# A retention block with a feed-forward block behind it: chunk 0's q loaded first, chunk 1 turned around chunk 0's products, chunk 8 turned by VectorE

## The chip, the cores and the metric

The kernel runs on one core of a Trainium2 chip. The metric is the device time of one execution in microseconds (us), lower is better, as the median of several runs. The core has five engines that run side by side, each with its own queue of instructions: TensorE (PE in the profile, with its weight loads as PEld), VectorE (DVE), ScalarE (ACT), GpSimd (POOL) and SyncE (SP), which here only issues transfers. Transfers (DMA) are also issued by ScalarE and GpSimd.

## What is computed

The inputs are q, k and v of 8 batches, 8 heads, 576 positions and 64 values each, a weight w_in of 512 x 2048 and a weight w_out of 2048 x 512, the weights in float64.

```python
scores = scale * np.matmul(q, k.transpose(0, 1, 3, 2))
gamma = 1.0 - 2.0 ** (-5.0 - np.arange(H))
Dmat = np.where(rel >= 0, gamma[:, None, None] ** rel[None, :, :], 0.0)   # rel = query position - key position
attn = np.matmul(scores * Dmat[None], v)             # (8, 8, 576, 64)
x = attn.transpose(0, 2, 1, 3).reshape(4608, 512)    # a row for each token
h = np.maximum(x @ w_in, 0.0)
out = h * h @ w_out                                  # (4608, 512)
```

## The kernel before

**Chunks.** The 4608 tokens are 36 chunks of 128, each of two halves of 64; nine halves make a sequence. A chunk's attention is: load q, k and v; scale q and v by powers of gamma (`scale_q`, `scale_v`); turn q and k, so that the head's 64 values lie along the partitions; multiply them to scores; mask the scores; multiply with v; add what a running state (k times v, summed over what came before) gives; and add this chunk to the state. The state is summed in a PSUM tile `u_ps`, and ScalarE copies it to `u_sb` after each half (`grown`, line 501) before the next half is added to the same tile (lines 538 and 568). The result of a chunk is copied to `room` as columns of x (line 550).

**Two ways of turning.** A chunk below `N_TURN` is turned by TensorE (`turn`: sixteen transposes, line 445, into two PSUM tiles, and two copies out, line 454, by ScalarE and VectorE or by ScalarE alone). A chunk from `N_TURN` on is turned by VectorE (`flip`): one transpose of k and one of q (line 416), each of which turns blocks of 32 x 32, and then sixteen copies of 32 x 256 on ScalarE (line 431), which put the blocks where they belong. The copies wait in a list, `moves`, and `move(count)` takes up to so many from it before each step.

**Order of the work.** Nothing is reordered: each engine runs what the program wrote for it in the order written. The first four chunks and parts of the next are written out by hand. They use `scores_full`, `carry_full` and `retain_full` on whole chunks. In between stands `convert`, which takes single operations of the weights' conversion from 64 bits to float32. A piece of w_in is 128 columns of it: `fetch_raw` issues its load of 512 KB, and six operations convert it: lines 227, 231, 238, 241 and 244 on VectorE, and line 235 on ScalarE, whose result line 241 needs. `first_in` (line 677) multiplies a converted piece with the first 512 tokens; there are sixteen of these, and ScalarE takes each result out of PSUM (line 683) and squares it (line 685). `warm` (line 845) is matmuls without a use.

**The chunk loop.** For each later chunk i, the loop first puts out what is left in `moves` for chunk i, then finishes the attention of chunk i - 1 (`whole`, lines 568, 574, 609, with the scores of the next chunk, line 480), turns chunk i + 1 if it is below `N_TURN`, scales its v on GpSimd, issues loads (`loads`), starts `flip` of chunk i + 2 if that is for VectorE, and then runs some feed-forward steps (`ffn`). Such a pass for i is called round i here. In rounds 5 to 8 the steps are three of `first_in`; before each, ScalarE gets `move`, then a piece is converted, and one of the pending transposes is put on VectorE. In `whole`, ScalarE copies the first half's state (line 501), and TensorE's next line 568 adds the following half to the same PSUM tile.

**Buffers.** q has three, k five and v four (`ld3`, `ld5`, `ld4`). A load waits for the last reader of the buffer that it takes. SP issues all loads in order, apart from chunk 0's k and v, which ScalarE issues.

**The rest.** From 95 us on TensorE works on the feed-forward blocks of 512 tokens with Strassen products (line 717), among the chunks, and from about 485 us on the second layer (line 1063). The change does not touch these.

Of the kernel before, what the change touches and what calls it, by code (L numbers as in the profile page):

```python
# [41 lines left out]
def kernel(  # L42
# [33 lines left out]
    nc = tc.nc  # L76
# [3 lines left out]
    HP = H // 2  # L80
# [10 lines left out]
    N_CH = n_tok // C  # L91
# [48 lines left out]
    def load(i, names="qkv"):  # L140
        if i == 0:
            nc.sync.dma_start(dv, decays)
        got = loaded.setdefault(i, [None] * 3)
        for name, pool, src in (("q", ld3, q), ("k", ld5, k), ("v", ld4, v)):
            if name not in names:
                continue
            t = got["qkv".index(name)] = pool.tile([128, H, D], F32, tag=name, name=f"{name}_ld")

            issue = nc.scalar if i == 0 and name != "q" else nc.sync
            b, c0 = divmod(i * C, S)  # L150
            runs = [(b, c0, slice(0, C))] if c0 + C <= S else [(b, c0, slice(0, CH)), (b + 1, 0, slice(CH, C))]
            for e in range(1 if name == "v" else 2):
                for b, c0, to in runs:
                    at = src[b, :, c0:c0 + to.stop - to.start, :].rearrange("h s d -> s h d")
                    if name == "v":
                        issue.dma_start(t[to], at)
                    else:
                        issue.dma_start(t[to, e * HP:(e + 1) * HP, :], at[:, e::2, :])
# [23 lines left out]
    def rows(half, n=64):  # L182
        return slice(64 * half, 64 * half + n)
# [21 lines left out]
    def fetch_w(j):  # L205
        if j < len(pieces) and wide:
            to = raw_of(j).bitcast(I64)
            if pieces[j][0] == 0:
                nc.sync.dma_start(to.rearrange("p (c f) -> p c f", c=N_DM), piece_src(j))
                return  # L210
            to = to.rearrange("p (o s b c) -> o s p b c", o=2, s=2, b=4)
            for o in range(2):
                for s in range(2):
                    nc.sync.dma_start(to[o, s], piece_src(j)[o, s])
# [94 lines left out]
    def fetch_raw(count):  # L309

        for _ in range(count):
            if n_raw[0] < min(N_W1, n_made[0] + N_RAW):
                fetch_w(n_raw[0])
                n_raw[0] += 1
# [18 lines left out]
    def convert(count):  # L333
        for _ in range(count):
            f = next(w_in_steps, None)
            f and f()
# [41 lines left out]
    def head(hp, e):  # L378
        return 4 * (hp % 2) + 2 * e + hp // 2

    HEADS = [(hp, e, hp // (HP // 2)) for hp in range(HP) for e in range(2)]
# [4 lines left out]
    def clears(half, bank):  # L386

        new = (half, bank) not in clean
        clean.add((half, bank))
        return new  # L390

    def scale_q(i, engine, parts=(slice(0, H),)):
        at = N_PAT + i % N_PAT
        for heads in parts:
            t = loaded[i][0][:, heads, :]
            engine.tensor_tensor(t, t, dv[:, heads, at:at + 1].to_broadcast(list(t.shape)), op=ALU.mult)  # L396
# [1 line left out]

    N_TURN = 9
    ps_t = [None]
    moves = []

    def new_qk(i):
        t = work3.tile([128, 2, HP, C], F32, tag="qk", name="qk")
        st[i]["qT"], st[i]["kT"] = t[:, 0, :, :], t[:, 1, :, :]
        return t
# [19 lines left out]
    def move(count, i=N_CH):  # L428

        while moves and count and moves[0][0] <= i and (moves[0][1] <= done[0] or count == C):  # L430
            nc.scalar.copy(*moves.pop(0)[2:])  # L431
            count -= 1

    def turn_in(i, js=(1, 0)):

        if "p" not in st[i]:
            if i < N_EARLY:
                p = [ps_e.tile([128, 512], F32, tag=f"e{h}", name="t_ps") for h in range(2)]
            else:
                p = [ps_f.tile([128, 512], F32, tag="f", name="t_ps") for h in range(2)]  # L440
            st[i]["p"] = [x.rearrange("p (j d t) -> p j d t", j=2, d=HP) for x in p]
        for j in js:
            for hp in range(HP):
                for h in range(2):
                    nc.tensor.transpose(st[i]["p"][h][:, j, hp, :], loaded[i][j][rows(h), 2 * hp:2 * hp + 2, :],  # L445
                                        ident[rows(h), rows(h)])

    def turn_out(i, engines=(0, 1)):

        p = st[i].pop("p")  # L450
        to = new_qk(i)
        copies = (nc.scalar.copy, nc.vector.tensor_copy)
        for h in range(2):
            copies[engines[h]](to[:, :, :, CH * h:CH * h + CH], p[h])

    def turn(i, engines=(0, 1)):
        turn_in(i)
        turn_out(i, engines)
# [41 lines left out]
    def grown(i, h):  # L500
        nc.scalar.copy(u_sb[(2 * i + h + 1) % 3], u_ps[0])
# [15 lines left out]
    def x_full(hp, e, b):  # L517
        return xp[0][rows(b), e, 0:256].rearrange("p (g t) -> p g t", g=2)[:, hp % 2, :]

    def carry_full(i):  # L520

        xp[0] = ps_x.tile([128, 2, 256], F32, tag="x", name="x_ps", padded_shape=[128, 2, 512])
        clean.clear()
        if i == 0:
            u_ps[0] = ps_u.tile([128, HP, D], F32, tag="u", name="u_ps")
            return
        u = u_sb[2 * i % 3]
        for hp, e, b in HEADS[0:2] + HEADS[4:6] + HEADS[2:4] + HEADS[6:8]:
            nc.tensor.matmul(x_full(hp, e, b), lhsT=u[rows(e), hp, :], rhs=st[i]["qT"][rows(e), hp, :],
                             start=clears(b, e), stop=False, skip_group_check=True)  # L530

    def retain_full(i):

        for hp, e, b in (HEADS[j] for j in (0, 4, 2, 6, 1, 5, 3, 7)):
            nc.tensor.matmul(x_full(hp, e, b), lhsT=st[i]["vs"][:, head(hp, e), :], rhs=st[i]["ret"][:, e, hp, :],  # L535
                             start=clears(b, e), stop=False, skip_group_check=True)
        for hp, e, b in HEADS:
            nc.tensor.matmul(u_ps[0][rows(e), hp, :], lhsT=loaded[i][1][:, 2 * hp + e, :], rhs=st[i]["vs"][:, head(hp, e), :],
                             start=(i == 0 and hp == 0), stop=(hp == HP - 1), skip_group_check=True)
        x_out(i, lambda: grown(i, 1))  # L540
# [256 lines left out]
    def step():  # L797
        n, f, *args = steps.pop(0)
        done[0] += 1
        f(*args)  # L800
        for _ in range(2 if len(transfers) > 2 else 1):
            if transfers and ahead[0] > QUIET:
                transfers.pop(0)[1]()
# [9 lines left out]
    def ffn(i):  # L813

        if steps and steps[0][0] == 0:

            for _ in range((N_W1 - N_EARLY) * C // TOK):
                move(4)
                convert(6)
                for f in flips[:1]:  # L820
                    f()
                del flips[:1]
                step()
            return
        count = N_MP * NP * C // TOK
        while steps and count:
            held[0] = count <= 1

            due = sum(m[0] <= i + 2 for m in moves)
            move(max(2, min(4, -(-due // (count - 1)))) if count > 1 else 0)  # L830
            ahead[0] = count
            busy[0] = len(flips) > 0
            for f in flips[:1]:
                f()
            del flips[:1]
            step()
            count -= 1
        held[0] = busy[0] = False
        ahead[0] = N_DF
# [6 lines left out]

    def loads(i):
        if i + 3 < N_CH:
            load(i + 3, "qk")
        if i + 2 < N_CH:  # L850
            load(i + 2, "v")

    halves = (slice(0, HP), slice(HP, H))
    warm(5)
    scale_q(0, nc.vector, halves)
    turn_in(0, (1,))
    scale_v(0)
    turn_in(0, (0,))
    turn_out(0)
    scale_q(1, nc.vector, halves)  # L860
    load(3)
    fetch_raw(3)
    warm(1)
    scores_full(0)
    turn(1, (0, 0))
    carry_full(0)
    retain_full(0)
    convert(3)
    scores_full(1)
    scale_q(2, nc.gpsimd)  # L870
    carry_full(1)
    retain_full(1)
    convert(3)
    turn(2, (0, 0))
    load(4)
    load(5, "qk")
    fetch_raw(1)
    load(5, "v")
    fetch_raw(1)
    first_in(0, (0,), (0, C))  # L880
# [26 lines left out]
    convert(3)  # L907
    scores(4)
    turn(5, (0, 0))
    load(7, "qk")  # L910
    scale_q(6, nc.gpsimd)
    convert(3)
    step()
# [1 line left out]
    for i in range(N_EARLY + 1, N_CH + 1):  # L915
        move(C, i)
        whole(i - 1)
        if i == N_EARLY + 1:
            convert(4)
        if i + 1 < N_TURN:  # L920
            turn(i + 1, (0, 0))
        if i + 1 < N_CH:
            scale_v(i + 1)
        loads(i)
        if N_TURN <= i + 2 < N_CH:
            flip(i + 2)
        ffn(i - 1)
        for j in range(n_scaled[0], min(i + (4 if i > N_TURN - 4 else 3), N_CH)):
            n_scaled[0] += 1
# [214 lines left out]
    for k in range(N_K + 1):  # L1144
        j = k % NP
# [81 lines left out]
```

## Time and profile before

| | |
|---|---|
| time, median of 3 runs | 931.64 us (931.31 to 931.79) |
| profiled execution | 931.4 us, of which the span of the profile is 929.7 |
| granted TensorE clock | 0.999 |
| PE busy | 922.7 us, 99% of the span |
| DVE, ACT, POOL busy | 756.2, 346.4, 84.3 us |
| ACT copies out of `flip` (line 431) | 432, 173.8 us, 402 ns each |
| DMA moved | 181.29 MB, 195 GB/s over the span |

Times in the views are microseconds from the start of the span. In a row of the timeline the start comes first, then the busy time, the engine, the line of the kernel, the operation, what it writes and reads, and how many instructions the row merges. In square brackets stands how long the engine was idle before it and what released it. TensorE's busy time is modelled at its end, since matmuls overlap, so that intervals between starts say more. Each float32 matmul is recorded twice. The DMA view gives, for the transfers issued in a stretch of time, the time from issue to landing.

### The profile page before, as it was taken

To read this page: it belongs to the slowest core of one execution; us is meant where nothing else is said; L and a number is where in the kernel's file an instruction comes from. 1 tells how busy PE (TensorE), PEld (TensorE's weight loads), DVE (VectorE), ACT (ScalarE), POOL (GpSimd) and SP (SyncE) were. 2 spreads that over 40 slices of the span, in tenths; PEclk is the share of its full clock that TensorE was granted. 3 is DMA by queue.
4 is the path that set the end of the run, shared out by engine and by line. 5 is a ranking of instruction groups with operands and counts; after the bars stand their busy time and mean duration, and the time that the engine had idled before them with its cause. 6 is when DMAs were issued, how large, how long until landed. Compare 5 with 4: busy or idle time off the path is not lost.

```text
span 929.7 us, 21073 instructions
## 1 busy us (share of the span) xinstructions
PE 922.7 (99%) x8548; PEld 830.3 (89%) x8548; DVE 756.2 (81%) x1215; ACT 346.4 (37%) x788; POOL 84.3 (9%) x84
## 2 busy tenths in 40 slices
PE   8999999999999999999999999999999999999998
PEld 7654888888888888888888899999999999999997
DVE  5888798888898888979876587878888888877887
ACT  3457767667676676676711110000000000000000
POOL 3322111121111111211000000000000000000000
PEclk9999999999999999999999999999999999999999
DMA  9998657678666785784379996566666575465523
GB/s 223 223 258 231 169 150 200 165 212 267 166 182 182 261 216 146 224 267 140 115 255 345 381 334 194 145 165 197 175 165 195 151 209 156 116 177 138 151 85 68
DMA packets 297152, 181.29 MB, mean 195 GB/s; under 512 B 194112, under 2 KB 270016, under 8 KB 296160
## 3 DMA queue, kind: packets, MB, share of 16 engines
q1 hardware_dynamic: 292064, 178.81, 66.4%
q10 hardware_dynamic: 4928, 1.08, 0.6%
q8 instruction: 67, 1.10, 0.5%
q14 instruction: 29, 0.24, 0.1%
q0 software_dynamic: 64, 0.07, 0.0%
HBM read 109.39 MB, written 70.52 MB: 194 GB/s over the span
## 4 chain that ended last, share of the span: by engine, by line
PE 98%; DVE 1%; issue 0%; POOL 0%; ACT 0%; POOLq 0%; DVEq 0%
PE h_b L717 18%; PE o_b L1063 17%; PE h_a L717 12%; PE h_c L717 12%; PE o_c L1063 12%; PE o_a L1063 12%; PE h_ps L677 6%; PE x_ps L574 3%; PE sc_ps L480 2%; PE x_ps L609 1%; PE u_ps L568 1%; PE idle_ps L845 0%; PE t_ps L445 0%; PE sc_ps L509 0%; PE x_ps L535 0%; DVE room L513 0%
## 5 line engine op out<-in xcount | busy, mean ns | idle before, releaser
L717 PE MATMUL h_b<-room,w 128*128 128x256 f32 x768 | 181.5, 379 | 0.0
L431 ACT COPY qk<-flip 32x256 f32<-32x256 f32 x432 | 173.8, 402 | 6.7
L717 PEld LDWEIGHTS h_b<-room,w 128*128 128x128 f32 x768 | 145.8, 190 | 20.0 <-DVE room L736 0.2
L717 PE MATMUL h_a<-room,w 128*128 128x256 f32 x512 | 123.9, 385 | 0.0
L717 PE MATMUL h_c<-room,w 128*128 128x256 f32 x512 | 121.0, 379 | 0.0
L717 PEld LDWEIGHTS h_c<-room,w 128*128 128x128 f32 x512 | 97.3, 190 | 13.2
L717 PEld LDWEIGHTS h_a<-room,w 128*128 128x128 f32 x512 | 95.0, 190 | 13.7
L1063 PE MATMUL o_b<-room,w 128*128 128x192 f32 x496 | 90.7, 326 | 0.0
L1076 ACT COPY r<-o_a 128x192 f32<-128x192 f32 x28 | 8.9, 319 | 209.4 <-PE o_a L1063 209.4
L1063 PEld LDWEIGHTS o_b<-room,w 128*128 128x128 f32 x496 | 82.3, 190 | 0.0
L724 DVE SCALAR_TENSOR_TENSOR room<-room 128x512 f32<-128x512 f32 x96 | 67.2, 700 | 3.3
L396 POOL TENSOR_TENSOR q_ld<-q_ld,dv 128x512 f32<-128x512 f32 x34 | 37.8, 1113 | 286.2 <-DMA q_ld<-in_q_dram 240.7
L1063 PE MATMUL o_a<-a,w 128*128 128x192 f32 x352 | 62.6, 326 | 0.0
L1063 PE MATMUL o_b<-s,w 128*128 128x192 f32 x336 | 61.5, 326 | 0.0
L1063 PE MATMUL o_c<-s,w 128*128 128x192 f32 x336 | 61.5, 326 | 0.0
L1063 PE MATMUL o_c<-room,w 128*128 128x192 f32 x336 | 61.5, 326 | 0.0
L677 PE MATMUL h_ps<-room,w 128*128 128x512 f32 (+1 forms) x152 | 57.7, 532 | 0.6 <-DVE w L244 0.5
L1063 PEld LDWEIGHTS o_a<-a,w 128*128 128x128 f32 x352 | 58.1, 190 | 0.1
L1063 PE MATMUL o_a<-room,w 128*128 128x192 f32 x320 | 56.9, 326 | 0.0
L1063 PEld LDWEIGHTS o_b<-s,w 128*128 128x128 f32 x336 | 55.8, 190 | 0.0
L1063 PEld LDWEIGHTS o_c<-s,w 128*128 128x128 f32 x336 | 55.8, 190 | 0.0
L1063 PEld LDWEIGHTS o_c<-room,w 128*128 128x128 f32 x336 | 55.8, 190 | 0.0
(117 smaller groups left out, 1412.6 us busy)
## 6 DMA issues: line engine op xcount, KB each, us to landing
g_dram<-room SPq DMA_DIRECT2D x164, 256.0 KB, 3.8
a<-g_dram SPq DMA_DIRECT2D x30, 512.0 KB, 5.8
room<-g_dram SPq DMA_DIRECT2D x28, 512.0 KB, 5.1
w_dram<-w SPq DMA_DIRECT2D x28, 448.0 KB, 4.4
w<-w_dram SPq DMA_DIRECT2D x7, 1792.0 KB, 9.6
q_ld<-in_q_dram SPq DMA_DIRECT2D x64, 128.0 KB, 4.1
w<-in_moe_w_in_dram SPq DMA_DIRECT2D x16, 512.0 KB, 6.0
w<-in_moe_w_out_dram SPq DMA_DIRECT2D x64, 128.0 KB, 3.4
```

The lines of the kernel that those rows point to most:

```text
L396: engine.tensor_tensor(t, t, dv[:, heads, at:at + 1].to_broadcast(list(t.shape)), op=ALU.mult)
L431: nc.scalar.copy(*moves.pop(0)[2:])
L480: nc.tensor.matmul(st[i]["sc"][e][rows(h), hp, :], lhsT=st[i]["kT"][rows(e), hp, t], rhs=st[i]["qT"][rows(e), hp, t], start=True, stop=Tru ...
L568: return [lambda hp=hp, e=e, b=b: nc.tensor.matmul(u[rows(e), hp, :], lhsT=loaded[i][1][rows(h), 2 * hp + e, :], rhs=st[i]["vs"][rows(h), ...
L574: return [lambda hp=hp, e=e, b=b: nc.tensor.matmul(x_at(hp, e, b, h), lhsT=s["vs"][rows(h), head(hp, e), :], rhs=s["ret"][rows(h), e, hp, ...
L609: m = nc.tensor.matmul(x_at(hp, e, b, h), lhsT=u[rows(e), hp, :], rhs=s["qT"][rows(e), hp, CH * h:CH * h + CH], start=clears(b, e), stop=F ...
L677: nc.tensor.matmul(p, lhsT=w[:, c, :], rhs=xT[0][:, c, :].rearrange("p (h t) -> p h t", h=2)[:, lo:hi, at[0]:at[1]], start=(c == 0), stop= ...
L717: nc.tensor.matmul(p[:, mm, :], lhsT=w[:, c, :], rhs=xs[n][right][:, c, :], start=(j in OPENS and mm == 0 and c == 0), stop=(j in CLOSES a ...
L724: nc.vector.scalar_tensor_tensor(t, t, 0.0, t, op0=ALU.max, op1=ALU.mult)
L1063: nc.tensor.matmul(p, lhsT=w_out[j][:, m, WO_SLOT[right], :], rhs=s["lefts"][left][:, m, :], start=(i in OPENS and m == 0), stop=(i in CLO ...
L1076: nc.scalar.copy(r[:, 0, LEFT], p)
```

## The change

Line numbers in this text are those of the kernel before; behind line 532 the changed kernel's are three higher, from the function `loads` on they differ a little more.

- Chunk 0: ScalarE issues q's two loads instead of k's two and v's one; SP issues k and v behind the decays.
- Chunk 1: VectorE scales half of q, GpSimd the other half. The sixteen transposes are split into two groups of eight: one directly behind chunk 0's scores, one between the fourth and the fifth of the eight products of chunk 0's scores with v. The two copies out go to ScalarE and VectorE instead of ScalarE alone. The first weight piece's six operations are placed two, two and two instead of three and three.
- The load of the fifth weight piece (piece 4) is issued before q, k and v of chunk 5 instead of behind its q and k.
- `loads` issues v with q and k of the same chunk, three chunks ahead; before, v came two chunks ahead. Chunk 7's v likewise.
- `N_TURN` is 8 instead of 9: chunk 8 is turned by VectorE. In rounds 5 to 8 up to five of the waiting copies precede each step instead of four.

```diff
-            issue = nc.scalar if i == 0 and name != "q" else nc.sync
+            issue = nc.scalar if i == 0 and name == "q" else nc.sync
...
-    N_TURN = 9
+    N_TURN = 8
...
-    def turn_in(i, js=(1, 0)):
+    def turn_in(i, js=(1, 0), hps=range(HP)):
...
-            for hp in range(HP):
+            for hp in hps:
...
-    def retain_full(i):
-
-        for hp, e, b in (HEADS[j] for j in (0, 4, 2, 6, 1, 5, 3, 7)):
+    def retain_full(i, inside=lambda: None):
+
+        for j in (0, 4, 2, 6, 1, 5, 3, 7):
+            hp, e, b = HEADS[j]
+            if j == 1:
+                inside()
...
-                move(4)
+                move(5)
...
         if i + 3 < N_CH:
-            load(i + 3, "qk")
-        if i + 2 < N_CH:
-            load(i + 2, "v")
+            load(i + 3)
...
-    scale_q(1, nc.vector, halves)
+    scale_q(1, nc.vector, halves[:1])
+    scale_q(1, nc.gpsimd, halves[1:])
     load(3)
     fetch_raw(3)
     warm(1)
     scores_full(0)
-    turn(1, (0, 0))
+    turn_in(1, (1, 0), (0, 1))
     carry_full(0)
-    retain_full(0)
-    convert(3)
+    retain_full(0, lambda: [turn_in(1, (1, 0), (2, 3)), turn_out(1), convert(2)])
+    convert(2)
     scores_full(1)
     scale_q(2, nc.gpsimd)
+    convert(2)
     carry_full(1)
     retain_full(1)
-    convert(3)
     turn(2, (0, 0))
     load(4)
+    fetch_raw(1)
     load(5, "qk")
-    fetch_raw(1)
     load(5, "v")
     fetch_raw(1)
...
-    load(7, "qk")
+    load(7)
```

## The prediction

> **What bounds the kernel now.** I read the page first: shares of busy time, then the chain that ended last.
>
> ```profile
> PE 922.7 (99%) x8548; PEld 830.3 (89%) x8548; DVE 756.2 (81%) x1215; ACT 346.4 (37%) x788; POOL 84.3 (9%) x84
> PE 98%; DVE 1%; issue 0%; POOL 0%; ACT 0%; POOLq 0%; DVEq 0%
> ```
>
> TensorE is the bound: a change can pay only where TensorE stands or does work it could leave out, and can hurt only where it makes TensorE wait. So I went through TensorE's rows in order of time.
>
> ```profile
> 6.17 0.89 PE L445 MATMUL t_ps<-w,q_ld 64*128 64x64 f32 x8
> 6.99 0.75 PE L845 MATMUL idle_ps<-w 128*128 128x256 f32 x2
> 7.97 1.16 PE L509 MATMUL sc_ps<-qk 64*128 64x128 f32 x16 [0.23 <-DVE qk L454]
> 10.10 1.16 PE L535 MATMUL x_ps<-room,v_ld 128*64 128x128 f32 x16 [0.21 <-DVE room L513]
> 13.69 1.16 PE L535 MATMUL x_ps<-room,v_ld 128*64 128x128 f32 x16 [0.27 <-DVE room L513]
> 16.55 1.16 PE L677 MATMUL h_ps<-room,w 128*128 128x128 f32 x8 [0.51 <-DVE w L244]
> ```
>
> All real waits lie before 17 us and are half a microsecond or less each. After that the timeline is dense, but one edge in it is tight: ScalarE's copy of the state (L501) and the next product into the same PSUM tile (L568), which must not start before the copy has read it.
>
> ```profile
> 41.38 0.37 ACT L501 COPY u_sb<-u_ps 128x256 f32<-128x256 f32 x1
> 41.61 0.28 PE L574 MATMUL x_ps<-qk,v_ld 64*64 64x64 f32 x4
> 41.90 0.27 PE L568 MATMUL u_ps<-v_ld,k_ld 64*64 64x64 f32 x2
> ```
>
> The copy ends at 41.75 and L568 starts at 41.90; later the pairs are 68.28 and 68.42, 81.54 and 81.69. It is always 0.14 to 0.15 us after the copy: if ScalarE is late there, TensorE is late by as much. This is ScalarE ahead of the third pair, in the round that the change touches:
>
> ```profile
> 77.08 0.60 ACT L683 ACTIVATE room<-h_ps 128x512 f32<-128x512 f32 x1 [1.65 <-PE h_ps L677]
> 77.58 1.63 ACT L431 COPY qk<-flip 32x256 f32<-32x256 f32 x4
> 79.23 0.72 ACT L235 ACTIVATE w<-w,exp_bias 128x512 uint32<-128x512 uint32 x1
> 79.86 0.61 ACT L685 ACTIVATE room<-room 128x512 f32<-128x512 f32 x1
> 80.51 0.60 ACT L683 ACTIVATE room<-h_ps 128x512 f32<-128x512 f32 x1
> 81.17 0.37 ACT L501 COPY u_sb<-u_ps 128x256 f32<-128x256 f32 x1
> ```
>
> A block-0 step takes TensorE 3.43 us (L683 starts at 73.65, 77.08, 80.51). ScalarE with four L431 copies, L235, L685 and L683 fills just that: no idle between 77.08 and 81.17. It has nothing left for a fifth copy.
>
> **What the Trainium skill says.** "PSUM — Partial Sum Buffer", section Engine vs sequencer instructions: ScalarE's and VectorE's queues are strict FIFO and matmuls start in program order. The rows above agree: L501 runs only after L683. So a moved copy delays all behind it. "VectorE: DVE Perf Modes", section The three transpose paths: VectorE transposes 32x32 blocks only. The trace agrees: each chunk turned so costs two transposes of 0.70 us and sixteen block copies (L431). "DMA: Bandwidth & Descriptors", section Issuing engines are not separate DMA queues: queues of SP and ScalarE share the same engines. The page's first slices show them 90% busy or more. "SBUF — State Buffer", section SBUF: two separate sides: VectorE and GpSimd exclude each other on a shared port. The trace fits: L231 takes 1.28 us instead of 0.42 at 57.04, beside GpSimd's row at 56.80.
>
> **The change, part by part.**
>
> *Chunk 0's q first.* Now q's second half lands at 6.08 (the DMA view: issued 1.74, 4.3 later), its scaling starts at 6.11, and TensorE's second half of q's transposes at 6.59. k sent by ScalarE at 0.80 and 1.30 landed at 3.49 and 4.77; q will land there. k on SP takes q's old place, behind the decays, but no v runs beside it: I estimate 5.2 (decays, q and k are 584 KB, 2.6 us at the first slice's 223 GB/s, from about 2.0, and half a microsecond of tail), at worst the old 6.08. TensorE can't begin before 5.69, where the warm-up matmuls end. So the 0.28 stall at 6.59 and some 0.13 of restart go: scores(0) moves from 7.97 to about 7.56. With k at 6.08 it gains 0.15.
>
> *Chunk 1 turned around chunk 0's products.* The bytes up to k1 are the same, so k1 still lands at 8.73 and 9.26. Half of q1's scaling leaves VectorE (0.4 us before the masks) for GpSimd. First masks at about 8.7 instead of 9.28, first products at 9.4, second half of the turn, second products, state: 0.5 + 0.4 + 0.5 + 0.6 gives scores(1) at 11.4 instead of 11.66. But step three of the weight piece (L238, 0.7 to 0.9) now stands before chunk 1's masks: 227 and 231 from 11.14, 238 until 12.8, masks at 12.8, where they started before (12.85). In return the piece is ready at 15.5 instead of 16.49. Chunk 2's k lands at 15.41 (issued 10.66, 4.75 later), and the turn of chunk 2 (15.25 now) can't pass it. It ends at 16.05 as before, first_in follows at 16.1 instead of 16.55, and scores(2) waits for ScalarE's two copies until 17.3 instead of 17.64. **Early gain: 0.34.** Bounds: 0 if k0 or q1 comes late, 0.65 if k2 lands without its tail.
>
> *Fifth weight piece ahead of chunk 5.* w4 landed at 35.92 and VectorE waited 0.51 for it, TensorE did not: its product starts at 43.4, and L244 of that piece ends at 40.1. With w4 ahead (2.3 us from 33.59 to 35.92), q5 lands at about 34.8 instead of 32.47 and k5 at 35.9; GpSimd scales q5 until 35.9, and the turn of chunk 5 wants k5 and q5 at 36.0 to 36.3. Nothing, with at most 0.5 of loss. Cover: four h_ps matmuls before it.
>
> *v with q and k.* v comes one chunk earlier; 256 KB, some 1.2 us, stand before the weights from w8 on. The tightest is piece 11: landed 61.94, used by L227 at 63.41; it becomes 63.1 against about 63.6. On SP, v now waits for the products of the chunk whose buffer it takes, just finished on TensorE; behind it stand stores of g, with buffers for two groups. Nothing; bound 0 to 0.5.
>
> *Chunk 8 turned by VectorE.* The chain shows what leaves TensorE:
>
> ```profile
> 69.34 0.64 PE t_ps L445 x16
> 69.98 10.50 PE h_ps L677 x24
> ```
>
> **Gain 0.64.** ScalarE loses two copies (1.09 at 70.06) and gets sixteen of 0.41 a chunk earlier, five a step instead of four. In order: chunk 8's are due 5 in the last step of round 6, then 5, 5 and 1 in round 7, where chunk 9's first 4 follow (now: 0, 0, 4).
>
> Round 6: L683 starts at 63.82 in the trace; + 0.50 + 5 x 0.41 + 0.63 + 0.52 to 0.65 gives the next at 67.5 to 67.7 against 67.25. L501 and so L568 slip by 0.2 to 0.4: **loss 0.3**.
>
> Round 7, from the start S of its first step: round 8 now shows first copies of L431 at S + 0.92 (83.45 against 82.53). Five copies until 2.98, L235 to 3.61, L685 to 4.13, L683 to 4.73, five copies to 6.79, L235 and L685 to 7.94, L683 to 8.54, one copy to 8.95. Chunk 9's copies wait for VectorE's transpose of q: its 241 waits for L235 (7.54), 244 follows at 8.27, the transpose at 8.88 to 9.58. Four copies until 11.3, L235 and L685 to 12.45, L683 to 13.0, then L501. Its present place is S + 10.5 + 0.76 = 11.26. **Loss 1.74**, 1.4 to 2.1 with the longer durations. There is no cover: L568 follows the copy directly. What is late next: nothing; TensorE's pause lets ScalarE catch up. In round 8 ScalarE ends its third step at about 10.8 against 10.4, and chunk 8's second half ends a sequence, so that no L501 comes before its products. VectorE's 1.4 us of new transposes in round 6 lie in its 1.94 idle at 67.2. Piece 12 is ready at S + 5.1 and wanted at 6.86.
>
> **Sum.** -0.34 - 0.64 + 0.3 + 1.74 = +1.06. The profiled execution took 931.4 (span 929.7), so 932.5; the median of the runs shown is 0.24 above it: **932.7**. Whatever moves before 95 us carries through: TensorE is dense to the end.
>
> **Rivals.** *ScalarE's copies stay hidden.* Then only gains are left: -0.98, 930.7. For it: ScalarE is 37% busy in all, and idles 1.36 and 1.65 in round 7. Against it: those 3.0 us, less 0.64 of shorter round, have to hold 15 copies in place of 4 and two wide ones, +3.4. *The start gains far more:* if chunk 2's data come before 14.8 and the copies stay hidden, -0.65 - 0.64 and some further tenths: 930.0, at best 929.5; only there is it faster. *The start gives nothing and the copies cost their upper bound:* 0.4 + 2.1 - 0.64 and 0.3 of waiting for q5 or k0 gives +2.2, 933.8, slower. It decides at L501 more than 2.5 us behind its present place.
>
> **How the numbers follow.** A measurement tells 0.2% (1.86 us) from no change. Likeliest case 62%, hidden copies 16%, large early gain 5%, upper bound with a lost start 17%. Slower by over 0.2% (above 933.5): the last and 8 of the first, 25%. Faster (below 929.8): 5%. Within: 70%. The range takes in the hidden copies and the upper bound: 930.6 to 934.2.
>
> **What would show it.** After: scores(0) near 7.6; the products of chunk 2's first_in near 16.1; no t_ps rows before the third round of h_ps; L501 of round 7 about 2.5 us after the h_ps matmuls of its block end instead of 0.76, with L568 0.15 behind its end; five L431 copies of 0.41 each. I am wrong if L501 keeps its place, if chunk 2's k lands much before 15.4, or if TensorE waits on q5, k5 or a weight piece in the stretch from 35 to 95 us.

## The result, and the profile after

The changed kernel takes 933.5 us (median of 14 runs, 932.51 to 936.25), the kernel before 931.33 us in the same comparison (931.07 to 932.03): a ratio of 1.0023, 95% interval 1.0016 to 1.0031. It is slower by 2.2 us. The interval, 1.5 to 2.9 us, leaves out no change at all, but it takes in the 1.86 us at which the prediction drew its line. The prediction was 932.7 (930.6 to 934.2). Of the single terms some are right and others wrong, as the traces show. The profiled execution of the changed kernel took 933.73, its span is 932.0 (before: 931.4 and 929.7).

First the page of the changed kernel, busy time and the chain that ended last:

```profile
PE 922.5 (99%) x8532; PEld 829.6 (89%) x8532; DVE 762.9 (82%) x1217; ACT 350.8 (38%) x801; POOL 86.4 (9%) x85
PE 94%; DVE 3%; DMA 1%; ACT 1%; issue 1%; POOL 0%; SPq 0%; POOLq 0%; DVEq 0%
```

TensorE's busy time is hardly less (the transposes that it lost are small). Of the chain 4% has gone from TensorE to others. That would be 37 us, and TensorE has lost 2.3: the chain says which way the last releases lead back, not how long TensorE stood. To see where it stood, TensorE's starts of the same matmul are laid side by side in both traces. A positive number means that the changed kernel is later there. The last column is the last matmul.

| matmul of the kernel before at (us) | 16.6 | 40 | 56.7 | 69.9 | 82.5 | 95.0 | 439 | end |
|---|---|---|---|---|---|---|---|---|
| changed kernel | +0.22 | +0.49 | +0.49 | -0.05 | +1.63 | +1.63 | +2.34 | +2.34 |

So four steps: +0.49 at the start, -0.54 in round 6 (0.64 of transposes saved, 0.10 lost), +1.68 at the end of round 7, and +0.71 in the Strassen part after 270 us. The start, in TensorE's, VectorE's and GpSimd's timeline of the changed kernel:

```profile
12.30 1.52 DVE L238 SCALAR_TENSOR_TENSOR w<-w,w 128x512 f32<-128x512 uint32 x1
13.74 1.27 DVE L513 TENSOR_TENSOR room<-sc_ps,room 128x512 f32<-128x512 f32 x2
12.21 1.06 POOL L495 TENSOR_TENSOR v_ld<-v_ld,dv 128x512 f32<-128x512 f32 x1 [3.56 <-DMA v_ld<-in_v_dram]
14.57 1.16 PE L538 MATMUL x_ps<-room,v_ld 128*64 128x128 f32 x16 [0.99 <-DVE room L513]
16.77 1.16 PE L680 MATMUL h_ps<-room,w 128*128 128x128 f32 x8
18.13 1.05 PE L509 MATMUL sc_ps<-qk 64*128 64x128 f32 x14 [0.21 <-ACT qk L454]
```

Scores of chunk 0 begin 0.26 earlier (7.71 for 7.97). But L238 takes 1.52 us, and not the 0.69 that it takes undisturbed, since GpSimd's scaling of v1 began just before it. The masks L513 wait behind it until 13.74 (before: 12.85), and chunk 1's products come at 14.57 instead of 13.69. The weight piece itself is then ready in good time: nothing waits at 16.77. Scores(2) at 18.13 wait for ScalarE's copies of chunk 2's turn, which the late products have delayed (before: 17.64).

Round 7 on ScalarE, and TensorE's next product:

```profile
79.56 1.65 ACT L431 COPY qk<-flip 32x256 f32<-32x256 f32 x4 [0.67 <-DVE flip L416]
81.23 0.72 ACT L235 ACTIVATE w<-w,exp_bias 128x512 uint32<-128x512 uint32 x1
81.86 0.61 ACT L688 ACTIVATE room<-room 128x512 f32<-128x512 f32 x1
82.38 0.58 ACT L686 ACTIVATE room<-h_ps 128x512 f32<-128x512 f32 x1
82.86 0.36 ACT L501 COPY u_sb<-u_ps 128x256 f32<-128x256 f32 x1
83.32 0.27 PE L571 MATMUL u_ps<-v_ld,k_ld 64*64 64x64 f32 x2 [1.46 <-issue]
```

The chain is as predicted: chunk 9's four copies wait for VectorE's transpose, all else queues behind them, L501 starts at 82.86, and TensorE follows 0.10 us after its end.

The last step, +0.71 after 270 us, starts at 261 us, with the scalings of v. First the kernel before, then the changed one:

```profile
261.36 1.06 POOL L495 TENSOR_TENSOR v_ld<-v_ld,dv 128x512 f32<-128x512 f32 x1 [1.66 <-DMA v_ld<-in_v_dram]
261.85 0.69 DVE L736 TENSOR_TENSOR room<-h_b,room 128x512 f32<-128x512 f32 x1 [0.59 <-PE h_b L717]
```

```profile
260.96 1.61 POOL L396 TENSOR_TENSOR q_ld<-q_ld,dv 128x512 f32<-128x512 f32 x1 [11.88 <-DMA q_ld<-in_q_dram]
261.57 1.28 DVE L227 TENSOR_SCALAR w<-w 128x512 uint32<-128x512 uint32 x1
262.53 1.23 POOL L495 TENSOR_TENSOR v_ld<-v_ld,dv 128x512 f32<-128x512 f32 x1
262.77 1.28 DVE L231 TENSOR_SCALAR w<-w 128x512 uint32<-128x512 uint32 x1
263.97 0.68 DVE L739 TENSOR_TENSOR room<-h_b,room 128x512 f32<-128x512 f32 x1
279.77 1.56 PE L720 MATMUL h_b<-room,w 128*128 128x256 f32 x6 [0.24 <-DVE room L739]
```

In the kernel before, the scaling of v waited 1.66 us for its data, and VectorE was through with L227 and L231 (0.41 and 0.42 us) before it; it even stood idle for 0.59. In the changed kernel v is there already, GpSimd scales q and v back to back, and L227 and L231 take 1.28 us each. L739 is then 2.12 later than L736 was in the kernel before, while TensorE is only 1.63 later. VectorE has no idle time in which to make this up, and at 279.77 TensorE waits for it. Between 275 and 279 us L238, L241 and L244 take 3.3 us together in both traces, so that nothing more is lost there. What is left of the 0.71 is lost at matmuls of h_b at 378 and 393 us, 0.2 and 0.1.

### The profile page after: what moved, and what is told of

Read it like the earlier page. It is cut to its first block, busy times and chain, and to the rows that moved or that the text cites. A ratio compares the mean times of both kernels' runs of the same rounds, so it can differ in the third digit from the quotient of the medians.

```text
span 932.0 us, 21034 instructions
## 1 busy us (share of the span) xinstructions
PE 922.5 (99%) x8532; PEld 829.6 (89%) x8532; DVE 762.9 (82%) x1217; ACT 350.8 (38%) x801; POOL 86.4 (9%) x85
## 4 chain that ended last, share of the span: by engine, by line
PE 94%; DVE 3%; DMA 1%; ACT 1%; issue 1%; POOL 0%; SPq 0%; POOLq 0%; DVEq 0%
PE o_b L1065 17%; PE h_b L720 17%; PE h_a L720 12%; PE o_c L1065 12%; PE o_a L1065 12%; PE h_c L720 11%; PE h_ps L680 5%; PE x_ps L577 3%; PE sc_ps L480 1%; PE x_ps L612 1%; PE u_ps L571 1%; DMA q_ld<-in_q_dram 1%; PE idle_ps L848 0%; PE t_ps L445 0%; PE x_ps L538 0%
## 5 line engine op out<-in xcount | busy, mean ns | idle before, releaser
L431 ACT COPY qk<-flip 32x256 f32<-32x256 f32 x448 | 180.3, 402 | 7.6 <-DVE flip L416 0.7
L396 POOL TENSOR_TENSOR q_ld<-q_ld,dv 128x512 f32<-128x512 f32 (+1 forms) x35 | 40.2, 1150 | 333.7 <-DMA q_ld<-in_q_dram 260.9
```

## The experiments

Each ran in five rounds beside the kernel before on the same chip. The ratio is to that kernel. Each expectation names a theory and a rival to it, with what either would show.

| kernel | time, us | ratio, 95% interval |
|---|---|---|
| chunk 8's turn alone | 932.89 | 1.0018 (1.0011 to 1.0024) |
| the same, chunk 9's copies later | 932.58 | 1.0013 (1.0005 to 1.0021) |
| the start alone (q first, chunk 1) | 931.52 | 1.0001 (0.9993 to 1.001) |
| v's loads alone | 933.22 | 1.0017 (1.001 to 1.0025) |
| all, chunk 9's copies later | 932.94 | 1.0018 (1.0011 to 1.0024) |
| all, L238 behind the masks | 933.63 | 1.0022 (1.0012 to 1.0033) |
| all but chunk 8's turn | 933.06 | 1.0019 (1.0011 to 1.0026) |
| all but v's loads | 932.57 | 1.0015 (1.0007 to 1.0024) |
| all, L686 behind L501 | 932.72 | 1.0013 (1.0005 to 1.0021) |
| all but the fifth weight piece | 933.65 | 1.0022 (1.0013 to 1.0031) |
| all, four warm-up matmuls | 934.37 | 1.003 (1.002 to 1.004) |
| the start alone, L686 behind L501 | 931.77 | 0.9999 (0.9991 to 1.0008) |

Intervals of neighbours overlap, so that a time alone seldom decides between two variants. The traces say more, but each is of one execution. TensorE's place against the kernel before, from one trace each, worked out as in the table above, follows with the time of the execution that was traced and the moment at which the trace's record has the TensorE clock rise (changed kernel: 6.79; before: 7.12):

| kernel | traced, us | clock up at | 16.6 | 40 | 56.7 | 69.9 | 82.5 | 95.0 | end |
|---|---|---|---|---|---|---|---|---|---|
| turn alone | 935.60 | 7.00 | +0.13 | +0.25 | +0.70 | +0.16 | +2.63 | +4.32 | +4.25 |
| turn alone, copies later | 932.29 | 5.67 | -0.22 | -0.21 | -0.16 | -0.08 | +0.29 | +1.00 | +0.93 |
| start alone | 931.72 | 5.08 | -0.97 | -0.60 | +0.26 | +0.26 | +0.26 | +0.26 | +0.32 |
| v's loads alone | 933.36 | 5.80 | +0.17 | +0.25 | +1.59 | +1.60 | +1.60 | +1.60 | +1.96 |
| all, copies later | 932.69 | 4.57 | -0.98 | +0.52 | +0.51 | +0.05 | +0.37 | +1.08 | +1.28 |
| all, L238 behind masks | 932.41 | 4.49 | -0.30 | -0.30 | -0.30 | -0.81 | +0.88 | +0.88 | +1.06 |
| all but the turn | 932.75 | 5.41 | -0.80 | +0.30 | +0.73 | +0.73 | +0.73 | +0.73 | +1.37 |
| all but v's loads | 932.55 | 3.96 | -0.93 | +0.13 | +0.13 | -0.42 | +1.28 | +1.28 | +1.19 |
| all, L686 behind L501 | 932.22 | 4.44 | -0.19 | -0.18 | -0.18 | -0.82 | +0.39 | +0.39 | +0.85 |
| all but the fifth weight piece | 939.66 | 6.99 | +1.16 | +2.27 | +3.16 | +2.61 | +5.87 | +7.56 | +8.23 |
| all, four warm-up matmuls | 932.49 | 3.96 | -0.46 | -0.46 | -0.43 | -0.61 | +1.08 | +1.08 | +1.08 |
| start alone, L686 behind L501 | 932.71 | 5.82 | -0.66 | +1.14 | +1.14 | +1.14 | +1.14 | +1.14 | +1.34 |

**Chunk 8's turn alone.**

```diff
-    N_TURN = 9
+    N_TURN = 8
...
-                move(4)
+                move(5)
```

> The kernel before with only the turn of chunk 8 moved to VectorE and up to five copies a step. Theory (ScalarE's copies push L501): t_ps rows of chunk 8 gone (-0.64 us), L501 of round 7 ends 1.6 to 1.8 us late and L568 starts 0.10 to 0.15 behind it, TensorE +1.1 us at 100 us against the kernel before, and the time +1.1. Rival (the slowdown of the whole change comes from its start alone): TensorE is 0.5 us early at 100 us and the time falls by 0.5.

Measured: 932.89, 1.4 us above before. Round 7 loses 2.47, more than in the whole change, since here VectorE's transpose comes later and the copies wait 1.41 for it instead of 0.67. The trace is of one of the kernel's long executions (935.6), and it shows a second loss, behind the stall:

```profile
84.31 0.27 PE L568 MATMUL u_ps<-v_ld,k_ld 64*64 64x64 f32 x2 [2.23 <-issue]
85.16 4.11 PE L677 MATMUL h_ps<-room,w 128*128 128x512 f32 x5
```

Five records of h_ps matmuls in 4.11 us: after the pause they start up to 0.86 us apart for about 3.4 us, then 0.43 again. That cost another 1.7 us and is taken up below. What follows: L501 behind the copies is the turn's cost, as predicted. The table shows one loss more that nobody had foreseen, 0.45 between 40 and 56.7 us, ahead of any copy: `N_TURN` also decides when GpSimd scales q. Chunk 8's q is scaled at 52.13 here, instead of 56.80, L227 (52.40) takes 1.28 us beside it, and L501 follows late. In the trace of the next run, with the same order on GpSimd, it cost only 0.05.

**The same with chunk 9's copies not before round 8.**

```diff
-moves.append((i, done[0] + (1 if steps[0][0] == 0 else 2), ...
+moves.append((i, done[0] + (1 if steps[0][0] == 0 and i != N_TURN + 1 else 2), ...
```

> As the turn of chunk 8 alone, but chunk 9's copies may not begin before round 8: the last step of round 7 has one copy in place of five. Theory (only the copies ahead of L501 in that step, and the wait for VectorE's second transpose of chunk 9, matter): L501 within 0.3 us of its old place behind the h_ps matmuls, TensorE 0.4 to 0.6 us early at 100 us, time -0.5. Rival (lateness piles up over all of round 7's steps): L501 stays 0.8 us or more late, time +0.3 or more.

The stall of round 7 fell to 0.34, as the theory had it, but the time did not: TensorE loses 0.7 us at 69 us, behind L501 of round 6, and 0.7 between 82.5 and 95, of which some 0.6 is a wait of L480 at 94.5 for chunk 9's copies, which now come too late for their user. So neither of the two places that were tried for these copies costs nothing.

**The start alone:** chunk 0's q first, and chunk 1 turned around chunk 0's products, as in the diff of the change.

> The kernel before with only chunk 0's q first and chunk 1's changes (half of q's scaling on GpSimd, the split turn, the weight piece's steps two, two and two). Theory (all that the start loses comes from these): first_in at 43.4 us starts 0.5 us late as in the changed kernel, and the time is +0.5. Rival (the start's loss comes from the transfers moved, the fifth weight piece and v): 0.1 to 0.3 us early, time -0.1 to -0.3.

The theory taken from the changed kernel's trace fell. Alone, the start gains 0.97 at first_in, still 0.60 at 40 us, and loses all of it at 55 us: L501 (54.91) is behind L686, which is behind L235, and that waits for VectorE's L227; TensorE's L571 stalls for 0.75. The time is that of the kernel before.

**v's loads alone.**

```diff
-            load(i + 3, "qk")
-        if i + 2 < N_CH:
-            load(i + 2, "v")
+            load(i + 3)
...
-    load(7, "qk")
+    load(7)
```

> The kernel before with only v loaded together with q and k, three chunks ahead. Theory (v lies ready when GpSimd has scaled q, so both scalings follow without a gap and hold VectorE's shared port twice in a row): TensorE is unchanged up to 270 us and then loses 0.3 to 0.7 us in waits for VectorE between 270 and 400 us; time +0.5. Rival (those waits come from VectorE's and ScalarE's new order after chunk 8): no wait there, time within 0.1.

933.22: alone this part costs 1.7 us, more than any other. The small later waits were foreseen (+0.36 after 95 us); the large one was not. GpSimd in the kernel before, then GpSimd, VectorE, ScalarE and TensorE in this one:

```profile
55.78 1.06 POOL L495 TENSOR_TENSOR v_ld<-v_ld,dv 128x512 f32<-128x512 f32 x1 [7.56 <-DMA v_ld<-in_v_dram]
56.80 1.24 POOL L396 TENSOR_TENSOR q_ld<-q_ld,dv 128x512 f32<-128x512 f32 x1
```

```profile
53.24 1.06 POOL L396 TENSOR_TENSOR q_ld<-q_ld,dv 128x512 f32<-128x512 f32 x1 [3.38 <-DMA q_ld<-in_q_dram]
53.27 1.31 DVE L227 TENSOR_SCALAR w<-w 128x512 uint32<-128x512 uint32 x1
54.62 0.72 ACT L235 ACTIVATE w<-w,exp_bias 128x512 uint32<-128x512 uint32 x1 [2.10 <-DVE w L227]
56.76 0.27 PE L568 MATMUL u_ps<-v_ld,k_ld 64*64 64x64 f32 x2 [1.08 <-ACT u_sb L501]
```

In the kernel before, the scaling of chunk 8's q stood in GpSimd's queue behind that of chunk 7's v, and v's data landed only at 55.71. With v loaded earlier, v is scaled at 48.81, where it holds up L244 (1.54 us instead of 0.69). And q is no longer held back: it is scaled as soon as its data are there, at 53.24, 3.56 us earlier than before, and falls on L227, which takes 1.31 us instead of 0.42. L235 waits 2.10 for L227, and L501 and L568 follow. The stall is 1.3 us. It is the same edge that chunk 8's copies hit, reached from another engine. That these meetings are the cause is read from the trace; no run moved GpSimd's scalings alone.

**Inside the whole change: chunk 9's copies later.** The same edit as above, in the changed kernel.

> The changed kernel, but the copies of chunk 9 are not due before round 8, so that only chunk 8's eleven copies stand in round 7's steps. Theory (the copies ahead of L501): the stall of 1.67 us before L571 at 83.3 shrinks to about 0.2, since four copies (1.65 us) leave the third step; the same four come up to 0.6 us late for the scores at 94 us, as they did when the change to chunk 8 was made alone. TensorE's end moves from +2.3 to +1.3 us against the kernel before, the time from 933.5 to about 932.5. Rival (the pause only moves): the copies are paid in full at their new place, and the end stays at +2.3 +- 0.3.

The stall at the end of round 7 is 0.3 instead of 1.67, TensorE's end +1.28, with a wait of some 0.6 at 94.6 for the late copies: the theory's numbers. The median is 932.94, between theory and rival. This trace also shows what the changed kernel's own trace doesn't: a start that gains.

```profile
5.17 0.71 PE L445 MATMUL t_ps<-w,k_ld 64*128 64x64 f32 x8
7.03 1.16 PE L509 MATMUL sc_ps<-qk 64*128 64x128 f32 x16 [0.28 <-DVE qk L454]
13.28 1.09 PE L538 MATMUL x_ps<-room,v_ld 128*64 128x128 f32 x16 [0.39 <-POOL v_ld L495]
```

The code up to here is that of the changed kernel, the transfers land at the same times (k's second half at 5.49, there 5.48), and still scores(0) start 0.68 earlier. The cause is in the warm-up matmuls ahead: here they are 0.43 us apart up to 4.27 and 0.22 from 4.64, in the changed kernel's trace 0.43 to their end at 5.69. TensorE's clock rises at another moment in each execution. Of the ten traces that have chunk 0's q first it rose between 3.96 and 5.41 us in seven, and only behind the end of the first warm-up, at 5.82 to 6.99, in three; scores(0) then start at 6.94 to 7.20 (7.48 where k landed late), or at 7.35, 7.71 and 7.71. In this trace the 0.68 us let L238 be through before GpSimd takes v1: it runs at 11.62 and takes 0.69.

**L238 behind chunk 1's masks.**

```diff
-    convert(2)
+    convert(1)
     scores_full(1)
     scale_q(2, nc.gpsimd)
-    convert(2)
+    convert(3)
```

> The changed kernel, but the first weight piece's L238 stands behind chunk 1's masks on VectorE instead of ahead of them. Theory (L238 beside GpSimd's scaling of v1 is what cost the start): the masks L513 start at about 12.3 instead of 13.74, chunk 1's products at 13.1 instead of 14.57, scores(2) at about 17.3 instead of 18.13, and TensorE stands 0.7 to 1.0 us earlier at 43 us. Rival (the gain at the start is not kept): VectorE, which converts the weights without a gap until 55 us, is late for its own reasons, L501 of the round that ends at 55 us follows it, and TensorE's end moves by less than 0.3 us.

The masks start at 12.23 and the products of chunk 1 at 13.07, as expected, but the time is the changed kernel's (933.63). The piece is ready later instead, and first_in at 16.25 waits 0.90 for L244. The trace is of the fastest of its eight executions, with an early clock, and there TensorE stands at -0.30 at 40 us, 0.79 ahead of the changed kernel's trace: what the theory said, but in the time nothing of it is left. How the other executions lose it isn't shown.

**All but chunk 8's turn, and all but v's loads.** The edits are the two above, undone in the changed kernel.

> The changed kernel, but chunk 8 is turned by TensorE and four copies precede a step, as before. Theory (chunk 8's copies cost 0.1 + 1.68 - 0.64 = 1.1 us): up to 65 us the same as the changed kernel (+0.5 us), no stall at 83 us, the end +1.2 us instead of +2.3, time about 932.4. Rival (the earlier loading of v is the larger part, as where it was made alone): a stall of 1 us or more before L571 near 56 us and an end of +2 us, time 933.2.

> The changed kernel, but v comes two chunks ahead behind the next chunk's q and k, as before. Theory (GpSimd's two scalings back to back hold VectorE): no step of +0.4 us at 280 us and none of +0.3 at 378 to 393, the end 0.7 us lower than the changed kernel's, time 932.8. Rival (the later steps are chance of how transfers fall): steps of the same sum elsewhere, the end within 0.3 us of the changed kernel's; or, if v's place decides where GpSimd meets the conversion of the weights between 45 and 60 us, a shift of 0.5 us or more there, in either direction.

Without the turn there is no stall at 83 us, but the time is 933.06, which is the rival's: v's loads alone had 1.0017, and 1.0019 is left. A stall of 0.41 at 55.9 is there, smaller than the rival's 1 us, and +0.64 after 95 us; the end of its traced execution, +1.37, is nearer to the theory's. Without v's loads it is 932.57, 0.9 lower than the changed kernel, with intervals that overlap. TensorE loses nothing between 95 us and the end (+1.28, then +1.19; the changed kernel +1.63, then +2.34), as the theory said. How much v's loads cost there differs from one trace to the next: 0.00 to 0.71 us in the eight traces that have them, -0.09 to +0.20 in the five that have v as before. The two parts don't add: alone they cost 1.4 and 1.7 us, and the whole change 2.2.

**L686 behind L501.** In rounds 5 to 8 ScalarE's copy of the third step's result is put behind the next L501.

```diff
-        nc.scalar.activation(t, p, AF.Relu)
+        if hold[0]:
+            held_out.append(lambda: nc.scalar.activation(t, p, AF.Relu))
+        else:
+            nc.scalar.activation(t, p, AF.Relu)
...
         if into:
             grown(i, 1)
+        if held_out:
+            held_out.pop()()
```

> The changed kernel, but in rounds 5 to 8 ScalarE's L686 of a round's third step (0.58 us) stands behind the next L501 instead of ahead of it; nothing else moves. Theory (TensorE's L571 follows ScalarE's queue at L501): L501 of round 7 comes 0.5 us earlier, the stall of 1.67 us becomes 1.15, TensorE's end moves by -0.5 to -0.7 us against the changed kernel, time about 932.9. Rival (the cost moves on): h_ps's buffer comes free later and the next round's first matmul waits for it by as much, time 933.5.

This was the sharpest test of the edge, since nothing but the order of two ScalarE instructions changes:

```profile
81.63 0.35 ACT L502 COPY u_sb<-u_ps 128x256 f32<-128x256 f32 x1
82.08 0.27 PE L572 MATMUL u_ps<-v_ld,k_ld 64*64 64x64 f32 x2 [0.97 <-issue]
```

(L502 and L572 are L501 and L571 of the changed kernel.) The stall is 1.19, for 1.67, where 1.15 was expected, and no later matmul up to 95 us waits in its place. Time 932.72, expected 932.9; its interval and the changed kernel's overlap a little.

**All but the fifth weight piece ahead of chunk 5.**

> The changed kernel, but the fifth weight piece's load stands behind chunk 5's q and k, as before. Theory (the piece ahead of chunk 5 takes back what the start gains): in the executions whose TensorE clock rises before 5.5 us, k of chunk 5 lands at about 35.2 instead of 36.2 to 36.9, the waits of 0.3 to 0.7 us ahead of chunk 5's transposes at 36 to 37 us go, and TensorE stands 0.3 to 0.5 us earlier at 43 us than before the change, where the changed kernel's variants stand +0.1 to +0.5; time about 933.0. Rival (the place of the piece costs nothing, as predicted): time 933.5, TensorE at 43 us no earlier, and VectorE waits for the piece instead.

The time is 933.65, with a ratio of 1.0022 for 1.0023: the rival, and the prediction's "nothing". Its traced execution was by far its longest (939.66) and is 1.16 us late already at 16.6, so the waits at 36 us can't be compared; it is of use for another reason:

```profile
81.08 1.51 POOL L495 TENSOR_TENSOR v_ld<-v_ld,dv 128x512 f32<-128x512 f32 x1
83.06 0.70 DVE L416 STREAM_TRANSPOSE flip<-q_ld 128x512 f32<-128x512 f32 x1
87.55 0.27 PE L571 MATMUL u_ps<-v_ld,k_ld 64*64 64x64 f32 x2 [3.02 <-issue]
```

Here GpSimd's scalings of q (80.06) and v came back to back while VectorE had L241 (1.51) and L244 (1.43) to do; the transpose is late, chunk 9's copies wait 2.23 for it, and TensorE stands for 3.0 us. So in this execution v's loads and chunk 8's turn meet at one point: v's make VectorE late, and the turn puts VectorE ahead of L501. They need not meet for a long stall: with the turn alone the copies waited 1.41.

**Four warm-up matmuls.** `warm(5)` became `warm(4)`.

> The changed kernel with four warm-up matmuls instead of five (0.43 us each at the slow clock). Theory (the last warm-up matmuls stand in the way when the clock rises late): chunk 0's transposes begin at about 4.9 instead of 5.69, scores(0) at 7.2 or before instead of 7.71, first_in at 16.0 or before instead of 16.77, time 0.3 to 0.5 us lower, 933.1. Rival (a gap behind the warm-up postpones the rise of the clock): scores(0) at 7.7 or later, and the time 933.5 or more.

934.37 is the slowest of all: the rival's side. Its traced execution, the fastest of the eight (932.49), had an early clock, so that the rival's mechanism, a gap that delays the clock, was not seen; why the kernel is slower stays open.

**The start alone, L686 behind L501.** The best candidate for a kernel faster than both.

> The kernel before with chunk 0's q first and chunk 1 turned around chunk 0's products (the part that ran at 931.52 us alone), and with L686 of each round's third step behind the next L501. Theory (the start's gain is lost where L501 stands behind L686): the stall of 0.75 us before L571 at 55.4 us shrinks to 0.2 or 0.3, TensorE keeps 0.2 to 0.5 us of the start's gain to the end, time 931.0 to 931.3, below the kernel before by less than 0.1%. Rival (VectorE is the limit there, and the loss moves on): the stall stands elsewhere before 95 us, time 931.5.

At 55 us L502 now waits for TensorE (0.80 us), not TensorE for it: that stall is gone. But the time is 931.77, the rival's, and the trace shows other waits before it:

```profile
24.71 1.16 PE L539 MATMUL x_ps<-room,v_ld 128*64 128x128 f32 x16 [0.83 <-DVE room L514]
```

The masks L514 stand on VectorE behind L227, which had waited 2.83 us for a weight piece; at 36.9 another 0.48 goes to scores behind VectorE's copy of a turn. A gain of 0.66 at first_in is +1.14 by 40 us. The trace is of one of its longer executions (932.71). None of the versions beats the kernel before by an amount that can be told.

## Why the prediction was right, and where it was not

**What bounds it.** Right in the main: TensorE was dense, and L501 was the tight edge before 95 us. It is where round 7, v's loads alone and the start alone lost most of their time. It was not the only place: once other engines run at other moments, TensorE also waits for chunk data (19 and 36 us), for masks (24.7) and for VectorE in the Strassen part (279.77). "Whatever moves before 95 us carries through" held; "TensorE is dense to the end" did not quite, since 0.71 was added after 270 us.

**Chunk 8.** Right. Round 7 was forecast to lose 1.74; the table gives 1.68 for the whole change and 1.69 or 1.70 in the three variants that kept this order (L238 behind the masks, without v's loads, four warm-ups). The inner steps are right too: L501 was forecast 13.0 us behind the start of the round's first h_ps step, and starts at 82.86, 13.0 behind 69.86; the wait of chunk 9's copies for VectorE's transpose, in the forecast 0.63, was 0.67. The saving of 0.64 came in full. Round 6 lost 0.10 for 0.3, and 0.0 to 0.7 over the nine traces with the turn. Together +1.14, forecast +1.40. Not foreseen was that `N_TURN` also moves GpSimd's scaling of chunk 8's q, which cost 0.45 in one trace and 0.05 in another.

**Chunk 0's q first.** Scores(0) were forecast at 7.56 and start at 7.71 in the traced execution. The landings came as estimated (q at 3.67 and 4.88, k at 5.48 for 5.2), and TensorE began at 5.69. The mis-sized term is "the 0.28 stall at 6.59 and some 0.13 of restart": 0.26 came of the 0.41. A further step failed in other executions: "TensorE can't begin before 5.69, where the warm-up matmuls end". That end was read from one trace as a fixed time. The Trainium skill, in "TensorE: Matmul & The Clock Gate", Part 1, says that the clock doubles after one busy window of some 3.4 us, and that the window runs freely, so that the moment differs from run to run. The traces agree: equal matmuls are 0.43 and then 0.22 us apart, and the clock rises at 3.96 to 7.12 us in the fourteen traces. With q first, scores(0) start as early as 6.94. In the four traces with the old order they start between 7.57 and 8.12; none of these has the clock up before 5.67, so what an early clock would give there is not shown.

**Chunk 1.** For the whole start the forecast was -0.34, and the trace has +0.49. The failed step is "238 until 12.8": L238 was given 0.7 to 0.9 us and took 1.52 beside GpSimd's v1, and ended at 13.8. The prediction had named the port that VectorE and GpSimd share, and GpSimd's row at 12.11 stood in the trace before; it was not laid over the new place of L238. Two smaller terms were off as well. Scores(1) were forecast at 11.4 and came at 11.82: in all ten traces with the new order they follow scores(0) by 4.1 us, for 3.84 in the forecast and 3.65 to 4.03 with the old order. And chunk 2's k landed at 14.54, not 15.41, one of the prediction's own signs of being wrong; the turn of chunk 2, at 16.12, then waited no longer for k but for TensorE's late products.

In executions with an early clock L238 is not hit, and first_in is up to 0.98 early, but this is not kept. Three of these traces (copies later, without the turn, without v's loads) show where it goes. There -0.80 to -0.98 has become +0.13 to +0.52 by 40 us: TensorE waits 0.4 to 0.5 for chunk 3's k at 19 us and 0.5 for chunk 5's at 36 us. In the start alone all of it is gone by 56 us. In the time, this part is worth nothing (1.0001 alone).

**Fifth weight piece.** "Nothing, with at most 0.5 of loss": right in the time, and the bound was reached. The wait for chunk 5's k in those three traces is 0.48 to 0.55 us; k lands at 36.95 in the first of them, at 33.59 in the kernel before. The prediction had named a wait on k5 as a sign of being wrong. In the changed kernel's own trace there is none: k landed at 35.93, and TensorE came at 36.84.

**v with q and k.** Wrong. "Nothing; bound 0 to 0.5" costed the transfers and SP's queue; it left out who uses v next. GpSimd scales v as soon as it lands and its queue is free, the scalings behind it move too, and their moments decide which instruction of VectorE takes two or three times its time. Alone the loads cost 1.7 us; in the changed kernel's trace +0.71, after 270 us.

**The sum.** Forecast +1.06: chunk 8 +1.40, start -0.34. Measured in the trace: +1.14, +0.49, and +0.71 for v's loads, +2.34. The mechanism that was argued for is the largest term; the other half of the loss comes from the start, forecast as a gain, and from v's loads, costed at nothing. That 933.5 still lies in the range is in part luck: its upper end was drawn for the copies at their upper bound with a lost start, not for v's loads.

## What to carry to other kernels

When a transfer is moved, follow it to the engine that takes its data first, and to what waits behind that in the engine's queue: here the load itself was hidden, and what cost time was GpSimd's scalings of v and of the q behind it, which ran at other moments and stretched instructions of VectorE. Where a short copy gates the bound engine, look at everything ahead of it in its queue and at what those wait for; several changes of quite different kinds can end at that one copy, and their costs then don't add. Look up, too, everything that a constant decides: `N_TURN` moved a scaling on a third engine. And a start that is read from one trace has the clock's phase in it: compare the warm-up matmuls before comparing starts.

## What the runs showed of the hardware

**A pause of TensorE can halve its clock.** After the pauses of 2.2 us (chunk 8's turn alone) and 3.0 us (without the fifth piece ahead) the h_ps matmuls started 0.85 us apart instead of 0.43, and 1.7 us were lost on top. The traces' records of the granted clock have half of it there for 3.41 us, from 85.50 and from 88.91. That is 78.51 and 81.92 us after the clock had risen, 23 and 24 times 3.41: in all fourteen traces the changes of the clock lie whole multiples of 3.413 us apart. In the step of 3.41 us before the fall TensorE had stood for 2.2 and 2.1 us. Steps with up to 1.5 us of standing, as with the pauses of round 7 in the other traces, were followed by no fall. The Trainium skill, in the page and part named above, gives an idle window of about 3.4 us as what lowers the clock; here a window that was idle for some 60 per cent of it did.

The execution's mean granted clock is 0.997 in both traces. Of the kernels that keep chunk 8's turn with chunk 9's copies in round 7, 8 of 89 executions have 0.998 or less; of the other kernels in the table none of 91, and of the kernel before 1 of the 141 beside the experiments. That fits some of the long executions that the changed kernel has and the one before has not; others above 934 us, without a lower clock, stay unexplained.

**Single instructions beside GpSimd.** L227 (128x512, uint32) took 1.28 to 1.31 us instead of 0.42, and L238 and L241 up to 1.5 instead of 0.69: each lost about 0.85 us, nearly the 1.06 of GpSimd's scaling. The scaling itself was stretched to 1.5 or 1.6 us where it was second. Not every meeting stretches VectorE: at 260.97 L640 took its 0.69 while the scaling that began with it took 1.61.
